# Other slots for the scores, denominators and means of three batches, and one batch's softmax product moved from VectorE to GpSimd

## The chip, the cores and the metric

One core of one Trainium2 chip runs the kernel. The metric is device time in microseconds, median of several runs. The profile is of one execution; its span is about 1.8 us shorter than the device time. PE is TensorE's matmuls, PEld its weight loads, DVE is VectorE, ACT ScalarE, POOL GpSimd.

## The reference

Linear attention over 32 memory slots for 8 batches of 8 heads, then a bilinear feed-forward layer on all 4,608 tokens:

```python
a = exp(phi); a = a / a.sum(over tokens)
k_m = einsum('bhsm,bhsd->bhmd', a, k);  v_m = einsum('bhsm,bhsd->bhmd', a, v)
attn = softmax(q @ k_m.T / sqrt(64))          # 32 columns
x = (attn @ v_m)                              # 4608 x 512
out = ((x @ w_a) * (x @ w_b)) @ w_out         # 512 -> 1536 -> 512
```

## The kernel before: the parts that matter

The kernel folds `v_m` into the two up weights (`vab = v_m @ w`), so that a batch's up products are `A @ vab` with `A` the normalised attention. TensorE is kept full by mixing three kinds of work: the up products of batch b (half steps of two `pa` and two `pb`), the down products of earlier batches (`work.advance`, lines `py`, `pv`, `px`), and the side units that make ready batch b + 1. The side units stand in a list; one slot of the list is run after each half step.

```python
def scores(gs): ...        # "sc": TensorE, 4 PSUM banks for two groups g
def exp_scores(g): ...     # "e":  ACT, E = exp(scores), frees two banks

def denominators(g):       # "den"
    t["L", g] = small.tile([P, S], F32, name="L")
    for hf in range(2):
        sl = slice(HALF * hf, HALF * (hf + 1))
        pD = banks.tile([P, HALF], F32, name="pD")
        nc.tensor.matmul(pD, ones, t["E"][:, g, sl], start=True, stop=True)
        nc.scalar.activation(out=t["L", g][:, sl], in_=pD, func=AF.Ln)

def normalise(g, hfs=slice(0, 2)):     # "nr": A = E * exp(-L)
    ...
    nc.scalar.activation(out=t["R", g][:, sl], in_=t["L", g][:, sl], func=AF.Exp, scale=-1.0)
    engine = nc.vector if b < 3 else nc.gpsimd
    engine.tensor_tensor(out=attn[b][:, g, sl], in0=t["E"][:, g, sl], in1=t["R", g][:, sl], op=ALU.mult)
...
# fold "v": TensorE, 4 banks pva;  take_fold "x": vab <- pva, group 0 on ACT, group 1 on DVE
# up_half: pa -> ACT a_sb;  pb -> DVE ht = a_sb * pb
# kv "kv": TensorE pkv; km "km": DVE rep (means of k and v); kvt "kvt": TensorE pT, DVE kvT; "qt": DVE transposes of q
...
def ups(steps, side=()):
    side = iter(side)
    for step in steps:
        for _ in up(*step):
            work.advance()
            next(side, us[step[0]]["-"])()
    for f in side:          # what is left of the list runs after the last step
        work.advance()
        f()
...
for b in range(2, B):
    if b == 2:
        load(4)             # four loads issued by POOL: phi, k, v, q
```

GpSimd also makes the sums of tokens (`h_sums`) for the down products, four of 128x768 per pair of chunks, and issues nearly all loads, batch 4's among them.

The softmax here doesn't subtract the row's maximum and nothing guards it: scores larger than these inputs give would overflow.

## Time and profile before

| | before |
|---|---|
| device time, median | 246.36 us at first; 246.31 with one more run |
| span of the profile | 244.6 us |
| TensorE busy | 233.6 us (95%) |
| idle of TensorE from 54 to 110 us | 2.07 us, of which 1.95 in the three stretches with a named wait |

The idle time is the sum of the stretches' lengths less TensorE's busy time in the table by stretch. From 110 to 210 us TensorE is never idle, so these waits are what a new order of side units can win. The prediction below shows the lines.

### The profile page before, as it was taken

How to read it: one execution, taken by the hardware profiler on the slowest of the kernel's cores; microseconds unless marked ns; L12 is line 12 of the kernel's file. 1: busy time of each engine (PE TensorE's matmuls, PEld its weight loads, DVE VectorE, ACT ScalarE, POOL GpSimd, SP SyncE). 2: the span in 40 equal slices, each digit the busy share in tenths (PEclk: the TensorE clock that was granted, in tenths of full speed). 3: DMA queues.
4: the chain of work that ended last, by engine and by line, in shares of the span. 5: the costliest groups of instructions: out<-in, count | busy, mean ns of one | idle time of the engine just before them, and what ended most of it. 6: DMA issues, size and time to landing. Idle time of an engine off the chain costs nothing.

```text
span 244.6 us, 7659 instructions
## 1 busy us (share of the span) xinstructions
PE 233.6 (95%) x3043; PEld 167.7 (69%) x3043; DVE 167.7 (69%) x403; ACT 157.2 (64%) x406; POOL 153.1 (63%) x128
## 2 busy tenths in 40 slices
PE   7979998999998999999999999999999999999993
PEld 2545654456666857767788777877787878888882
DVE  3536773568869868876994659865996576756642
ACT  2355761679697489578856768577856867565330
POOL 8722263499898029892899759892849177937001
PEclk9999999999999999999999999999999999999999
DMA  6999999999989704973159832696120403032154
GB/s 198 210 207 207 211 251 208 255 225 280 221 199 207 156 3 114 240 125 86 34 143 211 180 86 46 163 206 151 29 62 3 88 0 87 3 88 60 43 128 117
DMA packets 25044, 33.82 MB, mean 138 GB/s; under 512 B 1936, under 2 KB 19472, under 8 KB 25008
## 3 DMA queue, kind: packets, MB, share of 16 engines
q0 software_dynamic: 18288, 22.84, 50.3%
q1 hardware_dynamic: 6208, 9.70, 16.0%
q10 hardware_dynamic: 512, 0.79, 0.9%
q8 instruction: 24, 0.39, 0.7%
q14 instruction: 12, 0.10, 0.1%
HBM read 42.47 MB, written 9.44 MB: 212 GB/s over the span
## 4 chain that ended last, share of the span: by engine, by line
PE 77%; DMA 16%; DVE 3%; ACT 1%; issue 1%; POOL 0%; DVEq 0%
PE pa L591 18%; PE py L463 17%; PE pb L591 17%; PE pv L463 8%; DMA wo_sb<-in_moe_w_out_dram 7%; DMA wa_sb<-in_moe_w_a_dram 6%; PE pva L336 5%; PE px L463 4%; PE po L388 3%; DMA ht<-in_k_dram 2%; PE pkv L212 2%; PE pD L313 2%; PE pscore L291 1%; PE pT L241 1%; DVE A L324 1%
## 5 line engine op out<-in xcount | busy, mean ns | idle before, releaser
L602 DVE TENSOR_TENSOR ht<-a_sb,pb 128x288 f16<-128x288 f16 x168 | 73.1, 448 | 38.2 <-ACT a_sb L599 29.2
L591 PEld LDWEIGHTS <-vab 128*128 128x128 f16 x768 | 71.6, 98 | 28.2 <-issue 10.4
L599 ACT CAST a_sb<-pa 128x288 f16<-128x288 f32 x168 | 66.4, 406 | 28.0 <-PE pa L591 26.1
L591 PE MATMUL pa<-A,vab 128*128 128x288 f16 x384 | 75.8, 287 | 1.4 <-DVE A L324 1.0
L591 PE MATMUL pb<-A,vab 128*128 128x288 f16 x384 | 75.0, 286 | 0.3 <-ACT vab L348 0.3
L445 POOL TENSOR_TENSOR h_sums<-ht 128x768 f16<-128x768 f16 x28 | 45.9, 1641 | 37.8 <-DVE ht L602 37.3
L463 PEld LDWEIGHTS <-h_sums 128*128 128x128 f16 x384 | 37.4, 98 | 6.9 <-issue 0.4
L348 DVE CAST vab<-pva 128x512 f16<-128x512 f32 (+1 forms) x50 | 32.4, 663 | 3.3 <-PE pva L336 2.6
L348 ACT CAST vab<-pva 128x512 f16<-128x512 f32 (+1 forms) x50 | 27.9, 577 | 9.4 <-PE pva L336 9.3
L463 PEld LDWEIGHTS <-ht 128*128 128x128 f16 x288 | 28.2, 98 | 5.6 <-issue 0.4
L463 PE MATMUL py<-w_sums,h_sums 128*128 128x256 f16 x192 | 30.3, 272 | 0.0
L445 POOL TENSOR_TENSOR h_sums<-h_sums,ht 128x768 f16<-128x768 f16 x14 | 23.1, 1650 | 0.9
L445 POOL TENSOR_TENSOR h_sums<-ht,h_sums 128x768 f16<-128x768 f16 x14 | 23.0, 1643 | 1.0
L304 ACT ACTIVATE E<-pscore 128x288 f16<-128x288 f32 x32 | 11.4, 416 | 13.0 <-PE pscore L291 12.9
L324 POOL TENSOR_TENSOR A<-E,R 128x576 f16<-128x576 f16 x10 | 12.8, 1278 | 7.0 <-ACT R L322 6.8
L463 PE MATMUL py<-wo_sb,ht 128*128 128x256 f16 x96 | 16.0, 273 | 0.0
L463 PE MATMUL pv<-w_sums,h_sums 128*128 128x256 f16 x96 | 16.0, 272 | 0.0
L203 DVE STREAM_TRANSPOSE qT<-q_sb 128x288 f32<-128x288 f32 x32 | 14.3, 461 | 2.3 <-DMA q_sb<-in_q_dram 2.3
L470 ACT ACTIVATE u<-py 128x256 f32<-128x256 f32 x32 | 12.4, 388 | 5.2 <-PE py L463 4.9
L463 PE MATMUL py<-w_sums,ht 128*128 128x256 f16 x96 | 15.5, 272 | 0.1
L463 PE MATMUL px<-wo_sb,ht 128*128 128x256 f16 x96 | 15.4, 273 | 0.0
L314 ACT ACTIVATE L<-pD 128x288 f32<-128x288 f32 x32 | 11.5, 418 | 5.0 <-PE pD L313 4.7
(65 smaller groups left out, 274.0 us busy)
## 6 DMA issues: line engine op xcount, KB each, us to landing
out_dram<-o_sb SPq DMA_DIRECT2D x68, 128.0 KB, 2.4
kv_sb<-in_v_dram POOLq DMA_DIRECT2D x7, 576.0 KB, 10.4
phi_sb<-in_phi_dram POOLq DMA_DIRECT2D x7, 576.0 KB, 5.1
kv_sb<-in_k_dram POOLq DMA_DIRECT2D x7, 576.0 KB, 8.5
q_sb<-in_q_dram POOLq DMA_DIRECT2D x6, 576.0 KB, 13.1
wa_sb<-in_moe_w_a_dram POOLq DMA_DIRECT2D x3, 512.0 KB, 15.0
wb_sb<-in_moe_w_b_dram POOLq DMA_DIRECT2D x3, 512.0 KB, 16.2
wo_sb<-in_moe_w_out_dram POOLq DMA_DIRECT2D x3, 512.0 KB, 17.5
```

Source lines behind the costliest of these rows:

```text
L203: nc.vector.transpose(out=t["qT"][:, hp, :].bitcast(F32), in_=qs[b][:, hp, :].bitcast(F32))
L304: nc.scalar.activation(out=Ev[:, g, :, z, :], in_=pss, func=AF.Exp, scale=1.0 / (8.0 * CS))
L314: nc.scalar.activation(out=t["L", g][:, sl], in_=pD, func=AF.Ln)
L324: engine.tensor_tensor(out=attn[b][:, g, sl], in0=t["E"][:, g, sl], in1=t["R", g][:, sl], op=ALU.mult)
L336: nc.tensor.matmul(t["pva", lo, z][g][0][32 * j:32 * j + 32, 0:hi - lo], t["kvT"][64 * r:64 * r + 64, 4 + g, M * j:M * j + M], w_sbs[z][64 ...
L348: engine_copy(out=vabs[b][z][:, g, lo:hi], in_=pva[:, 0:hi - lo])
L445: engine.tensor_tensor(out=out, in0=in0, in1=in1, op=op)
L463: nc.tensor.matmul(po, lhs[:, i], rhs[:, i], start=first and i == 0, stop=i == KH - 1, skip_group_check=not first)
L470: nc.scalar.mul(out=x, in_=po, mul=scale)
L591: nc.tensor.matmul(ps, vabs[b][x][:, g, P * i:P * (i + 1)], attn[b][:, g, HALF * hf:HALF * (hf + 1)], start=(g == 0), stop=(g == 1))
L599: nc.scalar.copy(out=a_sbs[b, i, hf], in_=ps)
L602: nc.vector.tensor_tensor(out=ht[:, i, t0:t0 + HALF], in0=a_sbs.pop((b, i, hf)), in1=ps, op=ALU.mult)
```

## The change

Its intent: batch 2's two products `A` leave VectorE, its denominators are taken together one half step after the exponentials, and in the next list the means of k and v follow directly on their sums.

```diff
-            engine = nc.vector if b < 3 else nc.gpsimd
+            engine = nc.vector if b < 2 else nc.gpsimd
...
-    ups(half_steps(1, 1, 4), slots(2, "- kvt qt3 sc+e0+e1+den0 - nr0+den1+v0+x0a - - x0b+nr1 - v1+x1b x1a"))
-    second = "v2_+x2a_+exp0 x2b_ exp1 - qt0+kv+km - qt1+qt2 kvt+qt3 sc+e0 - e1+v0+x0a den0+x0b v1+x1a nr0+L x1b+exp0' den1 - nr1+v2+x2a - x2b+exp1' - qt0'+kv'+qt1' km' - qt2'+kvt'+qt3'"
+    ups(half_steps(1, 1, 4), slots(2, "- kvt qt3 sc+e0+e1 - den0+den1 nr0+nr1 v0+x0a x0b - v1+x1b x1a"))
+    second = "v2_+x2a_+exp0 x2b_ exp1 - kv+km qt0 qt1 kvt qt2+qt3 sc+e0 e1+v0+x0a den0+x0b v1+x1a nr0+L x1b+exp0' den1 - nr1+v2+x2a - x2b+exp1' - kv'+km' qt0'+qt1' - qt2'+kvt'+qt3'"
```

The first list serves batch 2; `second` serves batch 3, with `_` for what is left of batch 2 and `'` for batch 4. Below, A0 and A1 are batch 2's products for groups 0 and 1 (half of the heads each), and R0 and R1 their factors, made by ACT; the up products' matmuls come in pairs, the first with A0 and the second with A1. A bank is a PSUM bank: an eviction, the copy of a result out of it, frees it for the next matmuls.

## The prediction

> **What bounds the kernel now.** I read the busy shares first, then the waits of TensorE, then the chain around each of them, and last the timelines of DVE, ACT and POOL there. The first section of the page:
>
> ```profile
> PE 233.6 (95%) x3043; PEld 167.7 (69%) x3043; DVE 167.7 (69%) x403; ACT 157.2 (64%) x406; POOL 153.1 (63%) x128
> ```
>
> TensorE is busy for 233.6 of 244.6 us at full clock; no other engine passes 69%. Only its 11 idle us can be won by moving other work. The busy time by stretch says where they lie:
>
> ```profile
> 0.00:41.00 41.00, 36.59 (x523) 20.93 (x524) 22.87 (x57) 18.93 (x46) 19.55 (x31) 1.00 1.14 213
> ...
> 65.00:70.00 5.00, 4.45 (x74) 2.77 (x72) 2.71 (x7) 4.59 (x14) 4.92 (x5) 1.00 0.98 195
> 70.00:76.00 6.00, 4.96 (x61) 2.90 (x62) 5.51 (x11) 4.85 (x13) 5.83 (x6) 1.00 1.01 211
> ...
> 100.00:106.00 6.00, 5.64 (x76) 4.01 (x75) 5.39 (x16) 2.79 (x8) 5.18 (x4) 1.00 1.19 232
> ...
> 130.00:210.00 80.00, 80.00 (x1000) 61.78 (x999) 57.62 (x135) 57.92 (x154) 56.94 (x40) 1.00 0.46 96
> 210.00:245.00 35.00, 30.37 (x264) 25.52 (x262) 18.91 (x45) 14.11 (x37) 11.89 (x9) 0.99 0.34 76
> ```
>
> The second column is the stretch's length, the third TensorE's busy time. The head loses 4.4 us and the tail 4.6; the change touches neither. What it can reach is 0.55 us in 65 to 70, 1.04 in 70 to 76 and 0.36 in 100 to 106, or 1.95 us. TensorE's waits from 56 to 110 us name all three:
>
> ```profile
> PE pa L591 <- DVE A L324: 1.0, 1, 1.0
> PE pD L313 <- ACT E L304: 0.5, 1, 0.5
> PE pT L241 <- DVE rep L232: 0.4, 1, 0.4
> ```
>
> From 110 to 210 TensorE has no gap, so time won before should carry to the end. The largest wait in the chain that ended last, and its cause in the timelines of DVE and POOL:
>
> ```profile
> 71.63 0.45 DVE ht L602
> 72.08 0.60 DVE vab L348
> 72.70 1.46 DVE A L324
> 74.16 0.04 issue
> 74.20 0.28 PE pa L591
> ```
> ```profile
> 69.64 0.46 DVE L324 TENSOR_TENSOR A<-E,R 128x576 f16<-128x576 f16 x1
> ...
> 72.70 1.45 DVE L324 TENSOR_TENSOR A<-E,R 128x576 f16<-128x576 f16 x1
> ```
> ```profile
> 72.17 1.65 POOL L445 TENSOR_TENSOR h_sums<-ht 128x768 f16<-128x768 f16 x1
> 73.90 1.75 POOL L445 TENSOR_TENSOR h_sums<-h_sums,ht 128x768 f16<-128x768 f16 x1
> ```
>
> Batch 2's first product A took 0.46 us while POOL was issuing loads. The second began inside a POOL sum, took 1.45 and ended 0.33 after that sum; batch 2's first up product waited for it until 74.20.
>
> **What the Trainium skill says.** "SBUF — State Buffer", section "Who interferes with whom": a DVE instruction with two SBUF inputs contends with a GpSimd instruction that reads SBUF, and the one that comes second is fully blocked until the first is done. The trace agrees: 1.45 us against 0.46 for the same shape, ending just after the POOL sum. "GPSIMD Engine Reference", section "3.1 Elementwise — side-by-side cycle accounting": GpSimd takes about twice DVE's time for a float32 tensor_tensor. Here the trace decides, in float16: 1.28 us on POOL for batches 3 to 7 against 0.46 unblocked on DVE, 2.8 times. "TensorE: Matmul & The Clock Gate", section "Back-to-back issue gap": an isolated warm gap of N / 2.4 + 2.5 ns, 122 ns for 288 columns; the chain has two pa in 0.24 us. So a half step of four up products is 0.49 us here.
>
> **The change part by part.** A slot is a place in the list of side units; one slot follows each half step.
>
> 1. Batch 2's scores to products. Before: slot 3 scores, both exponentials and den0; slot 5 nr0, den1 and fold v0; slot 8 nr1. After: den0 and den1 in slot 5, nr0 and nr1 in slot 6, v0 in slot 7; products on POOL. Off TensorE at slot 3 goes the 0.55 us wait of pD for E. That is not won for itself: both orders run into the wait for A, so the end of A1 decides. ACT makes R, and before it is back to back from the first E at 66.47 to 73.91. Its set of work stays; only its order changes. Spacings from its starts: E 0.30, a_sb 0.35, L 0.29, R 0.60, u 0.30. After: 66.47 + 4 E (1.18) + 2 a_sb (0.69) = 68.34; + 4 L (1.17) = 69.51; + a_sb and u (0.65) = 70.16; + R0 = 70.76; + R1 = 71.36, landing near 71.45. Before, R1 ended at 72.67. POOL's four sums end at 69.22, so it is free: A0 from 70.9 to 72.2, A1 to 73.5. The up product that waited until 74.20 can start near 73.55: **-0.65 us**.
>
>  The folds move the other way. a_sb and the four evictions by ACT follow R1 and end near 73.9 as before. DVE no longer makes A: ht near 72.2, then four evictions of 0.64, ending at 74.75 instead of 75.34. The fold v1 needs banks from the first of these, so it ends near 73.3, just ahead of A1. I charge 0.1 us for banks: **net -0.55 us**.
>
> 2. POOL's queue behind. The two products take 2.56 us, and POOL first idles 1.7 us for R, so batch 4's four loads are issued from 73.5 instead of 69.17, and the next four sums start at 76.5 instead of 72.17 and end at about 83.3. Their first use before is at 83.9, their last after 89; each of the four is ready at least 3 us ahead. Loads: DMA is at 0.00 from 85 to 87 us, so 4.3 us later means landed by 89.3; batch 4's exp is made at 92.65. Cost: **0**.
>
> 3. Batch 3's scores one slot later, second exponential and v0 where they were. Before, there was an empty slot between; now half a step (0.49 us) is all that TensorE has ahead of v0, whose four banks include ones that E and a_sb must free. Before, ACT ran E, two a_sb, E, eviction in 86.27 to 88.05 and TensorE lost 0.08 us. With one a_sb fewer, fold v1 (bound by an a_sb eviction before, ending 90.6) ends 0.35 us sooner after the scores, but 0.49 us of up products has moved in front of them, and two fewer bank waits are covered. **+0.2 us**, an estimate.
>
> 4. km directly behind kv, transposes of q after it, for batches 3 and 4. Before, batch 4's kvt waits 0.36 us for rep. After, rep is done by about 101.8 and kvt has two more half steps and three more down products ahead: that wait goes. But DVE is gapless from 99.17 to 104.8 and its work is the same; the last transpose of q, which the scores need (a weight load of theirs waited for it at 104.70), stays near 104.5. So part comes back there: **-0.2 us**, not -0.36. An extra slot after batch 2's last step only moves down products forward.
>
> Sum: -0.55 + 0 + 0.2 - 0.2 = -0.55 us, from 246.36 to **245.8 us**.
>
> **The rivals.** (a) Everything in reach is won: no wait at the scores, A1 early, no wait for rep. For it: those waits are the only ones named and POOL had slack after 79. Against: ACT is full from 66.5 to 73.9, and A1 costs 1.28 us on POOL behind A0. It would be 244.4. (b) POOL becomes the bound: A1 comes later than I think because R is late (den1 waits for a bank held by up products, or ACT pauses). Each 0.3 us of it takes 0.3 us of the gain; at 0.65 nothing is left, 246.4, and with the closer packing of part 3 it is 246.8. For it: in 65 to 76 ACT and POOL are the fullest engines. (c) The late loads or sums stall TensorE at the fourth batch or second pair. Against: the margins of 3 us above. It would add 1 to 3 us, 247 to 249. (d) The gain is absorbed later by DVE, 4.93 of 5 us busy in 80 to 85. Against: TensorE has no wait in that stretch. It would be 246.2.
>
> **Range and chances.** Between (a), rather unlikely, and (b), quite possible, the range is 245.0 to 246.7. Faster by 2% needs -4.9 us, more than twice the idle in reach: 0.01. Slower by 2% needs something like (c) twice over: 0.02. Within 2%: 0.97.
>
> **What would show it.** Right: no DVE A after batch 1 and two POOL A of 1.28 us, the second ending near 73.5; the first up product of batch 2 with both halves near 73.55; batch 4's loads issued from about 73.5 with no wait for them; wait pT for rep gone; DVE still gapless before batch 4's scores, with a wait there for qT. Wrong: A1 after 74.1 (part 1), a TensorE wait over 0.5 us at v0 or v1 near 87 to 90 (part 3 too small), any TensorE wait traced to h_sums or to phi, k, v or q (part 2), or a new gap after 110, where I take time as carried through.

## The result, and the profile after

| | before | after |
|---|---|---|
| device time, median (4 runs each) | 246.31 us | 245.63 us |
| span of the profile | 244.6 us | 243.8 us |
| TensorE idle, 65 to 76 us | 1.59 us | 0.58 us |
| TensorE idle, 100 to 106 us | 0.36 us | 0.16 us |

The ratio is 0.9972, 95% interval 0.9955 to 0.9990. A ratio is the mean time of one kernel's fast runs over that of the other's in the same rounds, so not quite the ratio of the medians. That is 0.69 us less, between 0.25 and 1.1. The idle in the two stretches fell by more, 1.21 us. Not all of it was time won: from the first to the last of the marks told below, idle fell from 2.04 to 0.83 us, but busy time for the same matmuls rose from 44.10 to 44.50 (the profile models their ends). So the idle shows where the gain lies, and the marks how large it is: 0.81 us in this pair of profiles.

TensorE's waits of the changed kernel from 56 to 110 us; the columns are total, count and longest. None of the three named before is left, and what took their place is 0.2 us at a bank of fold v1:

```profile
PE pva L336 <- DVE vab L348: 0.2, 1, 0.2
```

The changed kernel by stretch (length, then busy time and count of PE, PEld, DVE, ACT, POOL, then clock, DMA share and GB/s):

```profile
65.00:70.00 5.00, 4.85 (x68) 3.42 (x66) 2.42 (x7) 4.59 (x16) 4.09 (x3) 1.00 1.00 197
70.00:76.00 6.00, 5.57 (x75) 3.09 (x73) 4.60 (x9) 5.55 (x14) 5.24 (x6) 1.00 0.20 38
...
100.00:106.00 6.00, 5.84 (x77) 4.23 (x76) 5.34 (x16) 3.52 (x10) 5.18 (x5) 1.00 1.20 227
106.00:110.00 4.00, 4.00 (x47) 2.84 (x45) 3.03 (x7) 3.32 (x10) 3.10 (x2) 1.00 0.42 79
110.00:130.00 20.00, 20.00 (x262) 15.72 (x260) 16.16 (x40) 13.96 (x36) 14.32 (x12) 1.00 0.45 100
```

TensorE is still gapless from 106 to 210, so what was won before is carried. POOL of the changed kernel, in order of time:

```profile
70.76 2.52 POOL L324 TENSOR_TENSOR A<-E,R 128x576 f16<-128x576 f16 x2 [1.60 <-ACT R L322]
73.21 0.80 POOL L78 DMA_DIRECT2D phi_sb<-in_phi_dram  x1
...
76.24 1.67 POOL L445 TENSOR_TENSOR h_sums<-ht 128x768 f16<-128x768 f16 x1
```

Both products end at 73.28; the loads and the token sums come 4 us later than before, and no TensorE wait is traced to them. The chain of the changed kernel where the wait for A was:

```profile
70.12 1.12 ACT R L322 x2
71.25 0.30 ACT a_sb L599
71.55 0.02 issue
71.57 0.46 DVE ht L602
72.03 0.61 DVE vab L348
72.64 0.04 issue
72.68 0.41 PE pva L336 x7
73.08 0.33 PE pv L463 x2
73.41 0.24 PE pa L591 x2
```

The chain no longer runs through A. It runs through ACT: both R stand ahead of the last a_sb, which holds back ht, the eviction behind it, and so a bank of fold v1. By the timeline the first pair of up products began at 73.25, its second half, which needs A1, at 73.37 (the two end 0.41 us after the first began, and one takes 0.29); A1 had ended at 73.28. So the path through ACT ended last, by at most 0.09 us: the two are almost equally long.

To see where the gain is, I cut the trace at groups that every version has: four last early down products (`po`) near 62 us, the sums kv of batch 3, fold v1 of batch 3, kv of batch 4 and fold v0 of batch 4. The times between their starts:

| us between | before | after | what lies there |
|---|---|---|---|
| po to kv of batch 3 | 17.27 | 16.45 | slots of batch 2, first up products of batch 2 |
| kv to v1 of batch 3 | 10.60 | 10.67 | scores of batch 3, moved by one slot |
| v1 of batch 3 to kv of batch 4 | 9.11 | 9.12 | nothing moved |
| kv to v0 of batch 4 | 9.16 | 9.09 | km, kvt, transposes of q, scores of batch 4 |

The marks in the chain, before and then after:

```profile
62.02 0.97 PE po L388 x4
79.29 0.87 PE pkv L212 x71
89.89 0.74 PE pva L336 x16
99.00 0.87 PE pkv L212 x72
108.16 0.56 PE pva L336 x16
```
```profile
61.96 0.97 PE po L388 x4
78.41 0.87 PE pkv L212 x72
89.08 0.74 PE pva L336 x16
98.20 0.87 PE pkv L212 x72
107.29 0.56 PE pva L336 x16
```

### The profile page after: what moved, and what is told of

Read it like the earlier page. It is cut to its first block, busy times and chain, and to the rows that moved or that the text cites. A ratio compares the mean times of both kernels' runs of the same rounds, so it can differ in the third digit from the quotient of the medians.

```text
span 243.8 us, 7661 instructions
## 1 busy us (share of the span) xinstructions
PE 233.6 (96%) x3043; PEld 167.9 (69%) x3043; DVE 166.0 (68%) x401; ACT 157.3 (65%) x406; POOL 155.6 (64%) x130
## 4 chain that ended last, share of the span: by engine, by line
PE 78%; DMA 16%; DVE 3%; ACT 1%; issue 1%; POOL 0%; DVEq 0%
PE pa L591 18%; PE pb L591 17%; PE py L463 17%; PE pv L463 8%; DMA wo_sb<-in_moe_w_out_dram 7%; DMA wa_sb<-in_moe_w_a_dram 6%; PE pva L336 5%; PE px L463 4%; PE po L388 3%; DMA ht<-in_k_dram 2%; PE pkv L212 2%; PE pscore L291 2%; PE pD L313 1%; DVE ht L602 1%; PE pT L241 1%
## 5 line engine op out<-in xcount | busy, mean ns | idle before, releaser
L324 POOL TENSOR_TENSOR A<-E,R 128x576 f16<-128x576 f16 x12 | 15.3, 1277 | 8.6 <-ACT R L322 8.3
L194 ACT ACTIVATE exp_sb<-phi_sb 128x576 f16<-128x576 f32 x16 | 11.0, 698 | 5.6 <-DMA phi_sb<-in_phi_dram 5.6
```

What stands on the lines that cost most here:

```text
L194: nc.scalar.activation(out=t["exp"][:, 2 * z:2 * z + 2, :, :], in_=phis[b][:, 2 * z:2 * z + 2, :].rearrange("p c (i m) -> p c i m", m=M), ...
```

## The experiments

Theory: the whole gain is that batch 2's first up product no longer waits for a VectorE product blocked by a reading GpSimd instruction; the slots let both products be made early, and the choice of engine matters little beside that. Rivals: (1) the engine carries the gain; (2) the wait at the scores was a loss of its own; (3) the long product has another cause than GpSimd's reads; (4) the slots of batches 3 and 4 bring a share. Each run is timed over five rounds against the kernel before on the same chip, and all gave right results.

The first four ran together; before was 246.27 us there.

**1. The engine alone.**

```diff
-            engine = nc.vector if b < 3 else nc.gpsimd
+            engine = nc.vector if b < 2 else nc.gpsimd
```

> The kernel before with batch 2's two products on POOL, all slots as before. Theory (ACT's order sets when A1 is ready, and the blocked read only adds to it): R1 still lands near 72.7, so A1 runs on POOL from 72.7 to 74.0 and the first up product of batch 2 goes on near 74.05 instead of 74.20; DVE is free of two products, so its evictions end sooner and fold v2 waits less: -0.2 to -0.4 us in all. Rival 1 (the block on DVE was the whole loss, the engine alone gives the gain): the wait of 1.0 us for A is gone and the time falls as in the full change, -0.7 us.

Measured: 246.01 us, ratio 0.9986 (0.9974 to 0.9999); po to kv 16.94 us, 0.33 less than before. TensorE's wait only changed its name:

```profile
PE pa L591 <- POOL A L324: 0.9, 1, 0.9
```

A1 ran on POOL from 72.65 to 73.92, because R1 was as late as before. Rival 1 falls as the whole cause: the engine alone gives 0.33 of the 0.82 us. What the trace offers for the 0.33 us is 1.27 us on POOL in place of 1.45 us blocked, and evictions on VectorE that no longer queue behind the product (three in one piece from 71.91 to 74.01).

**2. The slots alone.** The changed kernel with the product back on VectorE:

```diff
-            engine = nc.vector if b < 2 else nc.gpsimd
+            engine = nc.vector if b < 3 else nc.gpsimd
```

> The changed kernel with batch 2's two products back on DVE. Theory: the new slots have both products made between 70.8 and 72.0, when POOL issues batch 4's loads and reads no SBUF, so neither is blocked (0.46 us each); ht and the evictions on DVE come up to 0.4 us later than in the changed kernel; the first up product starts at 73.4 to 73.8; -0.4 to -0.8 us against before, so the slots carry the gain and GpSimd is not needed. Rival 1 (GpSimd carries it): one product is blocked again for about 1.4 us and the gain is gone, within 0.2 us of before.

Measured: 245.51 us, ratio 0.9969 (0.9957 to 0.9982); po to kv 16.52 us. Both products were made in one piece while POOL issued loads:

```profile
70.77 1.02 DVE L324 TENSOR_TENSOR A<-E,R 128x576 f16<-128x576 f16 x2 [0.40 <-ACT R L322]
```

So the slots alone give 0.75 of the 0.82 us that the trace shows for this stretch; the engine adds 0.07 with these slots. By time the two kernels cannot be told apart.

**3. Only the wait at the scores taken away.**

```diff
-  "- kvt qt3 sc+e0+e1+den0 - nr0+den1+v0+x0a - - x0b+nr1 - v1+x1b x1a"
+  "- kvt qt3 sc+e0+e1 den0 nr0+den1+v0+x0a - - x0b+nr1 - v1+x1b x1a"
```

> The kernel before with den0 alone moved one slot on, so that half a step of up products covers TensorE's wait for E. Theory: the wait of 0.55 us for E falls to 0.1 or less, the wait for A grows by as much, since ACT's order to R1 is nearly the same; time within 0.2 us of before. Rival 2 (the wait at the scores was a loss of its own): -0.4 to -0.6 us.

Measured: 246.19 us, ratio 0.9993 (0.9980 to 1.0007); po to kv 17.29 us, as before. The wait of 0.5 us for E is gone from the list, and the wait for A is 1.1 instead of 1.0; the chain lost the rest to banks at fold v0 and to a_sb. Rival 2 falls: time won ahead of a wait that something else ends is lost at that wait. My wording that this wait would grow by as much was too narrow, since part of it was lost earlier.

**4. The block alone taken away.** Before, with POOL kept busy by writes of an unused tile while VectorE makes A1:

```diff
         if b == 2:
             load(4)
+            for _ in range(4):
+                nc.gpsimd.memset(warm, 0.0)
```

> The kernel before with four GpSimd memsets of a tile that is no longer used, put between batch 4's loads and the next token sums, so that POOL writes but reads no SBUF while DVE makes A1; the result stays right. Theory (a DVE product with two SBUF inputs is blocked only by a POOL instruction that reads SBUF): A1 takes 0.46 us from 72.7 although POOL is busy, the up product goes on near 73.2 instead of 74.20, -0.7 to -1.0 us. Rival 3 (any POOL instruction blocks it, or the 1.45 us has another cause such as late R): A1 takes 0.9 us or more again, within 0.4 us of before.

Measured: 245.29 us, ratio 0.9960 (0.9947 to 0.9972); po to kv 16.28 us, 0.99 less than before and 0.17 less than the changed kernel.

```profile
72.07 2.30 POOL L698 MEMSET warm<- 128x512 f16 x4
72.63 0.46 DVE L324 TENSOR_TENSOR A<-E,R 128x576 f16<-128x576 f16 x1
```

The product takes its own 0.46 us inside 2.30 us of GpSimd writes. R1, the slots and the engine are those of before, so the block was the loss that mattered, and taking it away alone wins a little more than the change: it is the fastest version measured, though by time its interval overlaps that of the changed kernel.

The next four ran together; before was 246.07 us there.

**5. Batch 2's part of the change alone** (its list and the engine; `second` as before):

```diff
-            engine = nc.vector if b < 3 else nc.gpsimd
+            engine = nc.vector if b < 2 else nc.gpsimd
...
-  "- kvt qt3 sc+e0+e1+den0 - nr0+den1+v0+x0a - - x0b+nr1 - v1+x1b x1a"
+  "- kvt qt3 sc+e0+e1 - den0+den1 nr0+nr1 v0+x0a x0b - v1+x1b x1a"
```

> The kernel before with the changed slots of batch 2 and its products on POOL, batches 3 and 4 as before. Theory: this part is the whole gain; fold v2 of batch 2 ends 0.8 us sooner than before, as in the full change, and the time falls by 0.5 to 0.9 us. Rival (the slots of batches 3 and 4 bring a share of their own): less than 0.4 us here.

Measured: 245.52 us, ratio 0.9977 (0.9963 to 0.9990). The marks lie 16.45, 10.59, 9.12 and 9.16 us apart: the first as in the changed kernel, the others as before.

**6. The part of batches 3 and 4 alone** (`second` as in the change, the rest as before):

```diff
-    second = "... qt0+kv+km - qt1+qt2 kvt+qt3 sc+e0 - e1+v0+x0a ... - qt0'+kv'+qt1' km' - qt2'+kvt'+qt3'"
+    second = "... kv+km qt0 qt1 kvt qt2+qt3 sc+e0 e1+v0+x0a ... - kv'+km' qt0'+qt1' - qt2'+kvt'+qt3'"
```

> The kernel before with the changed slots of batches 3 and 4 alone. Theory, from the traces: 0.07 us lost from batch 3's scores to its fold v1 and 0.07 us won at batch 4's transpose, where TensorE's wait for rep is replaced by a wait for DVE's transposes of q: within 0.2 us of before. My prediction's terms gave 0.2 lost and 0.2 won, the same sum with larger parts. Rival as in the run of part 1: -0.3 us or more.

Measured: 246.20 us, ratio 1.0005 (0.9992 to 1.0017). The marks lie 17.27, 10.68, 9.11 and 9.10 us apart: 0.08 lost, 0.06 won. Rival 4 falls. TensorE's wait for `rep` is gone in both kernels that have this part. What took its place is in the chain of the changed kernel, ahead of batch 4's scores:

```profile
100.56 0.34 DVE rep L232
100.90 0.36 DVE ht L602
101.26 0.75 DVE qT L203 x2
102.01 0.18 DVE ht L602
...
102.66 0.53 DVE kvT L242
103.18 0.04 issue
103.23 0.68 PE pscore L291 x20
```

VectorE has the same work to do in either order. The wait that the profile names ahead of the scores is not one for a transpose of q, as the prediction and the expectation above have it: it is 0.4 us of a weight load for `kvT`, which in VectorE's order stands behind three of the four transposes.

**7. GpSimd kept busy with reads instead of writes.**

```diff
         if b == 2:
             load(4)
+            for _ in range(2):
+                nc.gpsimd.tensor_tensor(out=warm, in0=warm, in1=warm, op=ALU.add)
```

> As the run with the memsets, but POOL does two sums of an unused zero tile of 128x512 there: it reads SBUF. Theory: A1, asked for at 72.6, is blocked until the first of them ends (about 73.2) and is done 0.33 us later, near 73.6: about 0.95 us for A1, half of the time lost to the block comes back, -0.4 to -0.7 us, and clearly slower than with memsets. Rival (the memsets helped because they put off the token sums, not because they do not read): A1 takes 0.46 us and the time is that of the memsets.

Measured: 245.43 us, ratio 0.9975 (0.9962 to 0.9987); po to kv 16.70 us. A1 took 0.55 us, which is near the rival's 0.46, but this run doesn't test it: A0 took 1.25 us this time, A1 was asked for only at 72.73, and the first sum was nearly over. That the time lies in the expected range is luck. What was new here is A0:

```profile
68.89 0.77 POOL L78 DMA_DIRECT2D phi_sb<-in_phi_dram  x1
69.34 1.25 DVE L324 TENSOR_TENSOR A<-E,R 128x576 f16<-128x576 f16 x1
69.65 0.75 POOL L82 DMA_DIRECT2D kv_sb<-in_k_dram  x1
```

By the profile POOL did nothing then but issue loads.

**8. A version meant to beat both.** Products on VectorE, A1 early enough to run beside the issue of loads, and the changed end of batch 3's list:

```diff
-  "- kvt qt3 sc+e0+e1+den0 - nr0+den1+v0+x0a - - x0b+nr1 - v1+x1b x1a"
+  "- kvt qt3 sc+e0+e1 den0 nr0+den1+v0+x0a nr1 - x0b - v1+x1b x1a"
...
-  ... x2b+exp1' - qt0'+kv'+qt1' km' - qt2'+kvt'+qt3'"
+  ... x2b+exp1' - kv'+km' qt0'+qt1' - qt2'+kvt'+qt3'"
```

> A version meant to beat both: the kernel before, products on DVE, with den0 one slot on and nr1 two slots earlier, so that A1 runs while POOL issues loads and needs no dummy work, and the changed end of batch 3's list (kv and km of batch 4 together). Theory: A1 is made unblocked near 71.8, fold v2 ends 0.9 to 1.1 us sooner than before and batch 4's transpose gives 0.07 us: -0.9 to -1.2 us. If R1 ahead of the last a_sb on ACT delays fold v1 as in the changed kernel: -0.6 to -0.8 us.

Measured: 245.34 us, ratio 0.9967 (0.9955 to 0.9980); marks 16.45, 10.60, 9.12 and 9.10 us apart. A1 took 0.46 us from 71.84, but R1 again stood ahead of the last a_sb, and fold v1 waited for a bank as in the changed kernel: the second case of the expectation. By the marks it equals the change but for the 0.07 us at batch 3, which it does not lose; by time the two cannot be told apart.

The next two ran together; before was 246.23 us there.

**9. The reading instruction, timed to meet A1.**

```diff
         if b == 2:
             load(4)
+            nc.gpsimd.memset(warm[:, 0:256], 0.0)
+            nc.gpsimd.tensor_tensor(out=warm, in0=warm, in1=warm, op=ALU.add)
+            nc.gpsimd.memset(warm[:, 0:256], 0.0)
```

> The kernel with dummy POOL work again, timed so that A1 meets a reading instruction near its start: a memset of 128x256 (about 0.3 us), one sum of 128x512 (1.14 us, reads SBUF), a memset. Theory: the sum runs from about 72.4 to 73.5 us, A1, asked for near 72.65, ends about 0.3 us after it, so it takes 1.1 to 1.2 us against 0.46 beside the memsets; the up product of batch 2 goes on near 73.85; -0.2 to -0.4 us against before, slower than with memsets alone. Rival (reading does not matter): A1 takes 0.46 us.

Measured: 245.92 us, ratio 0.9986 (0.9971 to 1.0000); po to kv 17.04 us.

```profile
72.40 1.03 POOL L698 TENSOR_TENSOR warm<-warm 128x512 f16<-128x512 f16 x1
72.52 1.22 DVE L324 TENSOR_TENSOR A<-E,R 128x576 f16<-128x576 f16 x1
73.49 0.31 POOL L699 MEMSET warm<- 128x256 f16 x1
...
73.80 0.28 PE L591 MATMUL pa<-A,vab 128*128 128x288 f16 x1 [0.82 <-DVE A L324]
```

The sum ends at 73.43 and A1 at 73.74, 0.31 us later; in the kernel before the distance is 0.33. Nothing reads the sum's result, and the token sums are put off as in experiment 4. With a reading sum in that place the product is blocked, with memsets it isn't: rival 3 falls. A sum and a memset are also different instructions; no other kind that reads was tried.

**10. A second version meant to beat both.** A0 on GpSimd, A1 on VectorE, batch 2's slots of before, and the changed end of batch 3's list as in experiment 8:

```diff
-            engine = nc.vector if b < 3 else nc.gpsimd
+            engine = nc.vector if b < 2 or (b == 2 and g == 1) else nc.gpsimd
```

> A second version meant to beat both: the slots of batch 2 as in the kernel before, the product of group 0 on POOL and that of group 1 on DVE, and the changed end of batch 3's list. Theory: A0 runs on POOL from 69.7 to 71.0, where nobody waits for it, and pushes batch 4's loads to 71 to 74, so that A1 on DVE from 72.65 meets only the issue of loads and takes 0.46 us; the up product goes on near 73.1 as with the memsets; -0.9 to -1.1 us. If the issue of loads can block a DVE product as well (A0 took 1.25 us once, in the run with two dummy sums), A1 takes about 1.2 us and the gain is 0.2 to 0.4 us.

Measured: 246.14 us, ratio 0.9993 (0.9978 to 1.0007); po to kv 17.23 us. The main expectation failed, and the gain, 0.09 us between the medians, is below the 0.2 to 0.4 of the second case too. By the profile A1 met only the issue of loads, and still took 1.42 us:

```profile
72.34 0.75 POOL L85 DMA_DIRECT2D kv_sb<-in_v_dram  x1
72.60 1.42 DVE L324 TENSOR_TENSOR A<-E,R 128x576 f16<-128x576 f16 x1
73.08 0.75 POOL L90 DMA_DIRECT2D q_sb<-in_q_dram  x1
```

The last two asked whether it matters how far the issue of a load has come when the product begins; before was 246.35 us there.

**11. The split version with its loads put off.**

```diff
         if b == 2:
+            nc.gpsimd.memset(warm[:, 0:400], 0.0)
             load(4)
```

> The split version (A0 on POOL, A1 on DVE) with a memset of 128x400, about 0.45 us, ahead of batch 4's loads, so that A1, asked for at 72.60, begins some 0.55 us into the issue of a load (k, from about 72.05) instead of 0.26 us into one. New theory after the split version's A1 took 1.42 us: a DVE product is blocked by the issue of a load too, if it begins in the first part of the issue (0.26 us in), but not late in it (0.42 to 0.62 us in, seven products of 0.46 us in the other runs; one of 1.25 at 0.45 speaks against a sharp limit). It expects A1 of 0.46 us, the up product near 73.1 and -0.8 to -1.0 us. Rival (the issue of loads blocks whenever an earlier load still writes, or at random): A1 of 0.9 us or more again, within 0.4 us of before.

Measured: 246.33 us, ratio 1.0001 (0.9988 to 1.0015). A1 began 0.64 us into the issue of k and took 1.42 us again. The record already spoke against the theory: in experiment 2, A0 began at 70.77 us, 0.09 us into the issue of v, and was not held up.

**12. The kernel before with its loads put off a little.**

```diff
         if b == 2:
+            nc.gpsimd.memset(warm[:, 0:112], 0.0)
             load(4)
```

> The kernel before with a short memset of 128x112 (about 0.2 us) ahead of batch 4's loads, which moves A0's start, 0.47 us into the issue of the load of phi before, to about 0.25 us into it. The phase theory: A0 is blocked until 0.2 us after the issue of the next load ends and takes 1.2 to 1.5 us, as A1 did in the split version. Rival: A0 takes 0.46 us as in eight other profiles. A1 is asked for later than before and the token sums begin 0.2 us later; the time within 0.4 us of before either way.

Measured: 246.47 us, ratio 1.0007 (0.9994 to 1.0019). A0 began 0.35 us into the issue of phi, not the 0.25 aimed at, and took 0.46 us, as in seven other profiles (not eight). A1 met a token sum and took 1.58. The phase theory failed in experiment 11 and gets no help from this one. What stays open: ten of batch 2's VectorE products in these profiles ran beside the issue of loads in 0.46 us, and three (experiments 7, 10 and 11) took 1.25 to 1.42. The runs do not say what sets them apart: not how far the issue had come (0.09 to 0.65 us for the ten, 0.26 to 0.64 for the three), as far as the profile's rough spans on POOL can tell. That the issue of loads is what held up the three is likely, not shown.

## Why the prediction was right

The time, 245.63 us, lies in the range, 0.17 us below the prediction of 245.8. The gain by time is 0.68 us between the medians, with the interval told above; by the marks of the two profiles it is 0.81 from po to v0 of batch 4 (46.14 against 45.33 us), and the steps are compared by those. By its own steps:

1. **Batch 2's part, -0.55 us predicted.** The trace shows -0.82 and experiment 5 the same. The mechanism held: R1 landed at 71.24 (predicted 71.45), POOL's products ended at 73.28 (73.5), the waiting up product went on at 73.37 (73.55), fold v1 ended just ahead of A1. That the wait at the scores would win nothing by itself is shown by experiment 3. The term was too small by 0.27 us. ACT came 0.2 us sooner to the end of R1 than forecast (0.06 of it because this profile was that much earlier from 62 us on). The 0.1 us charged for banks was mis-sized: a wait of 0.19 us for a bank did come, at fold v1, but it ran beside the wait for A and can have cost at most the 0.09 us from A1's end to 73.37.
2. **POOL's queue, 0.** Right: loads were issued from 73.21 and sums made from 76.24, and no wait is traced to them.
3. **Batch 3's scores, +0.2.** A cost, as foreseen, but 0.07 us in the change and 0.08 in experiment 6. The estimate was too large.
4. **km and kvt of batches 3 and 4, -0.2.** The wait for rep went and came back ahead of the scores, as foreseen, but the wait there was for `kvT` and not for qT, and nearly all of it came back: -0.07 us in the change, -0.06 in experiment 6. The argument that VectorE's work is the same should have been followed to its end. The sum of steps 3 and 4 is right to 0.02 us by luck, because two errors of like size cancel.
5. **The rivals.** Full gain (a) was not reached; (b), (c) and (d) did not come about. The path that bounds the changed kernel, through ACT's order (R1, the last a_sb, ht, an eviction, a bank of fold v1), stands in part 1, but as ending just ahead of A1; in the trace what follows on it is the later, by at most 0.09 us. Experiment 4, which leaves ACT's order alone, was 0.17 us better in the same stretch.

Two of its sums are wrong and enter nothing else. Its last stretch runs to 245.00 us, beyond the span's end at 244.6, so the tail loses about 4.2 us and not 4.6. And the 246.8 of rival (b) does not follow: 246.4 and the 0.2 of part 3 make 246.6.

What the prediction took as given, that the long product came from GpSimd's token sum, which reads SBUF, is shown by experiments 4 and 9. That moving the product to GpSimd was needed for the cure is not: experiment 2 keeps it on VectorE and has nearly all of the gain.

## What to carry to other kernels

When an instruction takes three times as long as others of its form, look at what the other engines ran meanwhile. Keeping GpSimd off reads while the instruction ran was worth a little more here than moving the work (0.99 us against 0.82 in that stretch). A wait that lies ahead of a later wait ended by something else is worth nothing by itself. And moving work forward on one engine in its program order delays what stands behind it: here both R in front of one a_sb made a fold wait 0.19 us for a bank.

## What the Trainium skill lacked or had wrong

- "SBUF — State Buffer", section "Who interferes with whom": the rule that a VectorE instruction with two SBUF inputs contends with a GpSimd instruction that reads SBUF, and not with one that only writes, is borne out (1.22 and 1.45 us beside reads, 0.46 beside 2.30 us of memsets). It lacks how much of the blocked instruction is left when the other ends: 0.31 to 0.33 us here, less than its own 0.46, although it says that the second one blocks fully.
- The same section infers that such an instruction does not get into the way of descriptor generation. Three products of 1.25, 1.42 and 1.42 us beside nothing but the issue of loads, against ten of 0.46, speak against relying on that the other way round; the runs do not settle the cause.
- "GPSIMD Engine Reference", section "3.1 Elementwise — side-by-side cycle accounting", has the ratio to VectorE for float32 alone, about 2. In float16, 128x576, it was 1.28 us against 0.46, 2.8 times.
